# A distance table cut out of a shared buffer, and shorter declared form buffers, in a one-core attention + feed-forward kernel

## The chip, the cores and the metric

The kernel runs on one core of a Trainium2 chip. The metric is the device time of one execution in microseconds (us), as the median of several. A core has five engines that each take their own instructions in order: PE (TensorE, the matrix multiplier; its weight loads are shown as PEld), DVE (VectorE), ACT (ScalarE), POOL (GpSimd) and SP (SyncE, which here only issues transfers). They meet through semaphores: an instruction that waits holds up everything behind it on its engine.

## The reference

Sliding-window attention with a linear distance bias, for 8 batches, 8 heads, 576 positions and head size 64, followed by a two-matrix feed-forward layer with a squared ReLU:

```
scores = q @ k.T / sqrt(64)
scores = where(0 <= rel < 128, scores - slope[h] * rel, -1e9)     # slope[h] = 2**-(h+1)
attn   = softmax(scores);  x = (attn @ v), heads side by side     # 4608 x 512
out    = (max(x @ w_in, 0) ** 2) @ w_out                          # 512 -> 2048 -> 512
```

## The kernel before, in words

The 4608 rows are cut into nine chunks c of 512 columns, and the attention of a chunk into four couples (two heads each, p = 0 to 3). The feed-forward weights stay in SBUF in an "arena" of 16 places of 8 KB per partition (`w[f]`, f = 0 to 15: the first 4 KB for w_in, the other 4 KB for w_out, each split in a high and a low part so that a product is three matmuls).

**Stages.** In the start (to about 130 us) the weights are loaded and split and the first chunk is computed. Chunks 1 and 2 multiply directly (L318 and L356). From chunk 3 on, the first product uses a scheme with seven products of half size instead of eight (`product`, L410): its operands are sums of blocks of x, the "forms" B11, B21, B22, T1 to T4 (cast on ACT in L737, remainder on POOL through the helper `minus`, L341), and sums of blocks of the weights that come back from DRAM through a ring of five 2 KB buffers sum0 to sum4 (`load_sum`, L389). Forms of row 1 and some of row 0 lie in the first half of the odd places of the arena, whose w_in is no longer read then, while the second product (`second`, L356) goes on reading the w_out half of the same places.

**A couple.** PE computes scores into PSUM in a "visit" (L746, together with the values of an older couple, L767). DVE adds the distance table and takes row minima (`top`, L482). ACT takes the exponential (`exp`, L489), DVE the reciprocal of the sums (L503), POOL the normalization (`norm`, L514). DVE transposes blocks (L687), which go to DRAM (L693) and come back turned (L698) for the values of a later visit. From couple 8 on, one table of two heads serves all couples: before each couple ACT scales it in place by a power of two (`scale`, L206).

**Places.** In the last 24 KB per partition, `cst` holds the distance tables of all eight heads in 6 KB: heads 2 to 7 first, then heads 0 and 1, and `table` is the slice of the last 1.5 KB. When the tables of heads 2 to 7 are used up, their bytes are used again: the buffer sum0 ends in the first 1 KB of `cst`, and the buffer t30 (exponentials of a half couple, 3 KB) lies from byte 1536 to byte 4608 of it. So neither shares a byte with the slice `table`, but both share bytes with the declared tensor `cst`. The framework draws its waits between such named tensors. Every second couple uses t30 and t31, the others t0 and t1, which lie elsewhere.

**Order.** All engines have a written order that a planner makes with fixed costs and due times; it doesn't look at these waits.

Of the kernel before, what the change touches and what calls it, by code (L numbers as in the profile page):

```python
# [11 lines left out]
F32 = mybir.dt.float32  # L12
F32R = mybir.dt.float32r
# [8 lines left out]
B, H, S, D = 8, 8, 576, 64  # L22
# [48 lines left out]
CST = 128 + 192 * H  # L71
# [34 lines left out]
class Kern:  # L106
# [28 lines left out]
    def lay_out(self):  # L135
        parts = (
            ("x", 34816), ("pp", 8192), ("qk", 4608), ("v", 2560), ("t", 6144), ("h", 8192), ("r", 2048), ("o", 4096),
            ("y", 1024), ("t2", 3072), ("o2", 4096), ("qk2", 4608), ("h2", 4096), ("v2", 2560), ("cst", 6144),
        )
        self.nc.alloc_sbuf_tensor("rest", [128, sum(n for _, n in parts)], mybir.dt.uint8)  # L140
        at, self.home = self.nc.sbuf_base - sum(n for _, n in parts), {}
        for name, n in parts:
            self.home[name], at = at, at + n
        H = self.home
        many = lambda name, shape, dt, spots: Ring([self.at_byte(f"{name}{i}", shape, dt, a) for i, a in enumerate(spots)])
        self.lq = many("qk", [128, 1152], F32, (H["qk"], H["qk2"]))
        self.lv = many("v", [128, 5, 128], F32, (H["v"], H["v2"]))
        self.cst = self.at_byte("cst", [128, CST - 128], F32, H["cst"])
        self.table = self.cst[:, 1152:1536]
        self.tp = many("t", [128, 4, 192], F32, (H["t"], H["t"] + 3072, H["t2"]))  # L150
        self.op = many("o", [128, 2, 512], F32, (H["o"], H["o2"]))
        self.hp = many("h", [128, 2, 512], F32R, (H["h"], H["h"] + 4096, H["h2"]))
        self.hp.only(0, 1, 2)
        self.pp = many("pp", [128, 1024], F32, (H["pp"], H["pp"] + 4096))
        self.pp.only(0, 1)
        self.both = self.at_byte("both", [128, 2048], F32, H["pp"])
        self.r = self.at_byte("r", [128, 512], F32, H["r"])
        sums = H["t2"]
        self.r2 = self.at_byte("r2", [128, 512], F32, sums + 13312)
        self.u = self.at_byte("u", [128, 256], F32, sums + 15360)  # L160
        self.none = self.at_byte("none", [128, 256], F32, H["o2"])
        self.stage = self.at_byte("stage", [128, 4, 2, 256], F32R, sums)
        self.sr = many("sum", [128, 2, 256], F32R, [sums + i for i in (17408, 0, 2048, 4096, 6144)])
        self.sr.only(*range(5))
        self.o3 = self.at_byte("o3", [128, 512], F32, sums + 11264)
        self.o4 = self.at_byte("o4", [128, 2, 512], F32, sums + 13312)
        self.t3 = [self.at_byte(f"t3{i}", [128, 4, 192], F32, sums + at) for i, at in enumerate((19968, 8192))]
        dense = lambda name, slot, shape, dt: self.at_byte(name, shape, dt, H["x"] + 2048 * slot)
        self.xs = {(c, p): dense(f"x{c}{p}", 9 * c + 2 * p, [128, 2, 512], F32R) for c in range(2) for p in range(NP)}
        names = [(n, row) for row in range(2) for n in ("B11", "T1")] + [(n, 0) for n in ("B21", "B22", "T2", "T3", "T4")]  # L170
        odd = lambda f: self.arena + 8192 * f
        spots = [[H["x"] + 2048 * i for i in range(9)], [H["x"] + 2048 * (9 + i) for i in range(6)] + [odd(f) for f in (1, 3, 5)]]
        self.forms = [{}, {}]
        for c in range(2):
            for name, spot in zip(names, spots[c]):
                self.forms[c][name] = self.form(f"{name[0]}{name[1]}_{c}", spot)
        for i, n in enumerate(("B21", "B22", "T2", "T3", "T4")):
            self.forms[0][n, 1] = self.forms[1][n, 1] = self.form(f"{n}1", odd(2 * i + 7))
        two = lambda name, spot: self.at_byte(name, [128, 2, 256], F32, spot)
        self.far = [two(f"far{i}", H["x"] + 2048 * (15 + i)) for i in range(2)]  # L180
        self.tt = self.at_byte("tt", [128, 3, 256], F32, H["o"])
        self.near_x = two("now", H["o"] + 3072)

    def form(self, name, spot):
        if spot < self.home["x"]:
            return self.at_byte(name, [128, 2, 2, 512], F32R, spot)[:, 0, :, 0:256]
        return self.at_byte(name, [128, 2, 256], F32R, spot)

    def join(self, ctx):
# [9 lines left out]
        self.low, self.big = (ctx.enter_context(self.tc.tile_pool(name=n, bufs=1, space=PSUM)) for n in ("low", "big"))  # L199

    def near(self, h):
        h = (h - 2) % H
        return self.cst[:, 192 * h : 192 * (h + 1)]

    def scale(self, p):
        self.nc.scalar.activation(self.table, self.table, AF.Copy, scale=2.0**-2 if p else 2.0**6)  # L206
# [8 lines left out]
        self.nc.gpsimd.memset(self.tiny, 1e-9)  # L215

    def distances(self):
        self.nc.sync.dma_start(self.cst, self.cstd[:, 128:CST])

    def widen(self, p, queue=None):  # L220
        a = CST + 512 * p
# [1212 lines left out]
```

## Time and profile before

| what | us |
|---|---|
| median of 3 runs (lowest, highest) | 909.11 (907.0, 910.17) |
| the profiled execution's own time | 909.9 |
| its span, first to last instruction | 908.0 |
| PE busy | 867.9 (96%) |
| DVE, ACT, POOL busy | 464.0, 439.0, 454.5 |

The profile comes from one execution. A busy PE is the matmuls' own time, so the idle time between them is what waits cost; the granted TensorE clock is given as a share of 2.4 GHz. "Idle before <- X" in a row is the time the engine stood still just before the instruction, and the instruction whose end let it go.

### The profile page before, as it was taken

To read this page: it belongs to the slowest core of one execution; us is meant where nothing else is said; L and a number is where in the kernel's file an instruction comes from. 1 tells how busy PE (TensorE), PEld (TensorE's weight loads), DVE (VectorE), ACT (ScalarE), POOL (GpSimd) and SP (SyncE) were. 2 spreads that over 40 slices of the span, in tenths; PEclk is the share of its full clock that TensorE was granted. 3 is DMA by queue.
4 is the path that set the end of the run, shared out by engine and by line. 5 is a ranking of instruction groups with operands and counts; after the bars stand their busy time and mean duration, and the time that the engine had idled before them with its cause. 6 is when DMAs were issued, how large, how long until landed. Compare 5 with 4: busy or idle time off the path is not lost.

```text
span 908.0 us, 20552 instructions
## 1 busy us (share of the span) xinstructions
PE 867.9 (96%) x7644; PEld 776.8 (86%) x7648; DVE 464.0 (51%) x1492; ACT 439.0 (48%) x1195; POOL 454.5 (50%) x480
## 2 busy tenths in 40 slices
PE   8899999999999999998999989999999799999998
PEld 5688887888888898887999879888889699999997
DVE  6999964122323245555665445645555455434342
ACT  7898865555665554444444333434444444223111
POOL 4312115798896555565456445555446534543222
PEclk9999999999999999999999989999999899999999
DMA  9995465445656357664667647665766555734331
GB/s 339 403 330 196 140 175 181 141 153 179 226 190 221 117 178 241 202 205 154 203 225 227 199 160 234 201 206 183 253 202 208 172 162 193 224 134 142 111 111 47
DMA packets 95651, 176.39 MB, mean 194 GB/s; under 512 B 9088, under 2 KB 35008, under 8 KB 95552
## 3 DMA queue, kind: packets, MB, share of 16 engines
q1 hardware_dynamic: 85264, 165.31, 55.1%
q10 hardware_dynamic: 10288, 9.77, 3.6%
q8 instruction: 61, 1.00, 0.5%
q14 instruction: 38, 0.31, 0.1%
HBM read 135.07 MB, written 39.98 MB: 193 GB/s over the span
## 4 chain that ended last, share of the span: by engine, by line
PE 60%; DVE 8%; ACT 5%; POOL 5%; DMA 3%; issue 2%; SPq 0%; ACTq 0%; DVEq 0%; POOLq 0%
PE acc L356 28%; PE g L410 11%; PE s L410 8%; PE g L318 7%; DVE t L482 5%; PE s L767 3%; DMA sum<-sums 3%; PE g L746 3%; ACT t L489 3%; POOL h L341 2%; DVE both L687 2%; PE s L746 1%; POOL t L514 1%; POOL T L341 1%; POOL B L341 1%
## 5 line engine op out<-in xcount | busy, mean ns | idle before, releaser
L356 PE MATMUL acc<-h,w 128*128 128x512 f32 x1728 | 418.9, 386 | 9.9 <-POOL T L341 9.9
L356 PEld LDWEIGHTS acc<-h,w 128*128 128x128 f32 x1728 | 329.4, 199 | 44.2 <-POOL T L341 10.7
L341 POOL TENSOR_TENSOR h<-r,h 128x512 fp32r<-128x512 f32 x128 | 167.6, 1311 | 160.9 <-ACT h L439 143.2
L318 PE MATMUL g<-x,w 128*128 128x512 f32 x576 | 133.9, 382 | 5.9 <-ACT r L324 4.0
L489 ACT ACTIVATE t<-t,nm 128x192 f32<-128x192 f32 x256 | 114.4, 448 | 44.5 <-DVE nm L482 40.4
L318 PEld LDWEIGHTS g<-x,w 128*128 128x128 f32 x576 | 107.4, 189 | 25.5 <-ACT r L324 7.7
L482 DVE CUSTOM_DVE_ANT_0 t<-g,cst 128x192 f32<-128x192 f32 (+4 forms) x192 | 56.9, 313 | 136.2 <-PE g L746 125.4
L439 ACT CAST h<-r 128x512 fp32r<-128x512 f32 x96 | 59.2, 617 | 117.2 <-PE acc L356 76.0
L514 POOL TENSOR_TENSOR t<-t,nm 128x768 f32<-128x768 f32 x57 | 86.3, 1515 | 34.5 <-DVE nm L503 32.4
L410 PE MATMUL g<-B,w 128*128 128x256 f32 x576 | 81.1, 277 | 6.1 <-ACT u L419 6.1
L410 PEld LDWEIGHTS g<-B,w 128*128 128x128 f32 x576 | 76.0, 192 | 10.7 <-ACT u L419 8.2
L410 PE MATMUL s<-T,sum 128*128 128x256 f32 x576 | 80.4, 276 | 3.8 <-ACT cst L206 2.3
L434 DVE SCALAR_TENSOR_TENSOR r<-r 128x512 f32<-128x512 f32 x96 | 78.7, 820 | 7.3 <-ACT r L427 1.5
L410 PEld LDWEIGHTS s<-T,sum 128*128 128x128 f32 x576 | 75.1, 191 | 7.5 <-ACT cst L206 3.1
L417 DVE TENSOR_TENSOR u<-s,u 128x256 f32<-128x256 f32 x48 | 20.3, 422 | 104.4 <-PE s L410 98.7
L417 DVE TENSOR_TENSOR r<-g,u 128x256 f32<-128x256 f32 x96 | 40.6, 423 | 29.5 <-PE g L410 14.3
L687 DVE STREAM_TRANSPOSE both<-t 128x768 f32<-128x768 f32 x56 | 51.4, 955 | 2.1 <-PE s L767 2.0
L767 PE MATMUL s<-both,v 64*64 64x64 f32 (+1 forms) x1648 | 50.1, 243 | 0.2
L482 DVE CUSTOM_DVE_ANT_0 t<-s,cst 64x192 f32<-64x192 f32 (+4 forms) x142 | 41.3, 298 | 14.0 <-ACT t L489 10.8
L489 ACT ACTIVATION_READ_ACCUMULATOR t<-t,nm 128x1 f32 x256 | 48.0, 187 | 0.0
L341 POOL TENSOR_TENSOR tt<-now,far 128x256 f32<-128x256 f32 x12 | 8.8, 735 | 75.7 <-ACT now L725 75.7
L410 PE MATMUL g<-B,sum 128*128 128x256 f32 x288 | 40.8, 278 | 5.1 <-DVE r L417 4.0
(113 smaller groups left out, 1144.1 us busy)
## 6 DMA issues: line engine op xcount, KB each, us to landing
sum<-sums SPq DMA_DIRECT2D x192, 256.0 KB, 3.8
both<-way SPq DMA_DIRECT2D x28, 1024.0 KB, 6.9
raw<-in_dram SPq DMA_DIRECT2D x32, 512.0 KB, 7.9
qk<-in_dram SPq DMA_DIRECT2D x32, 320.0 KB, 3.1
v<-in_dram SPq DMA_DIRECT2D x32, 320.0 KB, 3.9
qk<-in_dram SPq DMA_DIRECT2D x36, 256.0 KB, 3.8
way<-both SPq DMA_DIRECT2D x56, 160.0 KB, 3.3
way<-both ACTq DMA_DIRECT2D x56, 160.0 KB, 3.5
```

Of the source, the lines that this page charges most:

```text
L318: nc.tensor.matmul(g, w, in_turn(xs[cc][:, part]), start=i == 0, stop=i == 11)
L341: return self.nc.gpsimd.tensor_tensor(to, a, b, op=op)
L356: self.nc.tensor.matmul(self.acc[m], w, in_turn(h), start=(f == 0 and i == 0), stop=(f == NF - 1 and i == 2))
L410: nc.tensor.matmul(to, w, in_turn(t[:, part]), start=i == 0 and k in (1, 5, 6, 7), stop=i == 5, skip_group_check=True,)
L417: V, add = nc.vector, lambda to, a, b: nc.vector.tensor_tensor(to, a, b, op=ALU.add)
L434: V.scalar_tensor_tensor(r, r, 0.0, r, op0=ALU.max, op1=ALU.mult)
L439: nc.scalar.copy(both[:, 0], r)
L482: self.nc.vector.tensor_tensor_reduce(self.t[r, m, a:e], spot, table[r, a:e], -0.125, least, ALU.add, ALU.min, to,)
L489: e = self.nc.scalar.activation(self.t[:, m], self.t[:, m], AF.Exp, bias=nm[:, m : m + 1], scale=-1.0, accum_out=nm[:, 4 + m : 5 + m],)
L514: self.nc.gpsimd.tensor_tensor(self.t, self.t, rec.unsqueeze(2).to_broadcast([128, 4, 192]), op=ALU.mult)
L687: nc.vector.transpose(squares[:, :, s].rearrange("p b m c -> p m b c"), G.t.rearrange("p m (b c) -> p m b c", c=32))
L767: made.append(mm(to, w, x, start=first and n < 2, stop=not first, skip_group_check=True))
```

## The change

The tables of heads 0 and 1 become a tensor `table` of their own, at the same bytes as the slice before, with their own load; `cst` is declared with 1152 columns, which end where t30 ends. The forms in the arena's odd places are declared 4 KB long instead of 8 KB, at the same bytes.

```diff
-        self.cst = self.at_byte("cst", [128, CST - 128], F32, H["cst"])
-        self.table = self.cst[:, 1152:1536]
+        self.cst = self.at_byte("cst", [128, 1152], F32, H["cst"])
+        self.table = self.at_byte("table", [128, 384], F32, H["cst"] + 4608)
...
         if spot < self.home["x"]:
-            return self.at_byte(name, [128, 2, 2, 512], F32R, spot)[:, 0, :, 0:256]
+            return self.at_byte(name, [128, 2, 512], F32R, spot)[:, :, 0:256]
...
     def near(self, h):
-        h = (h - 2) % H
-        return self.cst[:, 192 * h : 192 * (h + 1)]
+        table, h = (self.table, h) if h < 2 else (self.cst, h - 2)
+        return table[:, 192 * h : 192 * (h + 1)]
...
     def distances(self):
-        self.nc.sync.dma_start(self.cst, self.cstd[:, 128:CST])
+        self.nc.sync.dma_start(self.table, self.cstd[:, 1280:CST])
+        self.nc.sync.dma_start(self.cst, self.cstd[:, 128:1280])
```

The instructions of PE, DVE, ACT and POOL keep their order; SP has one transfer more. What differs is for what they wait. A row is one instruction with what it writes and reads; in brackets are the semaphores it waits for (DMAHWn is a transfer). Lines of the changed kernel are one higher.

On ACT, the stretch of the couple that is scored at 507 us. Before:

```order
L419 COPY u<-g 128x256 [waits PE_49]
L693 DMA way<-both 32x5x256 [waits DMAHW4_49,DMAHW6_49,DMAHW3_49,DVE_49]
L693 DMA way<-both 32x5x256 [waits DMAHW7_49]
L737 CAST T_133<-tt 128x256 [waits PE_49,Pool_49]
L489 ACTIVATE t_104,nm<-t_104,nm 128x192 x2
L206 ACTIVATE cst<-cst 128x384 [waits DMAHW0_49,Pool_49]
L427 ACTIVATE r<-g 128x256 [waits PE_49]
L737 CAST B_131<-now 128x256
L499 ACTIVATE nm<-nm,tiny 128x4 [waits Activation_49]
L737 CAST T_134<-tt 128x256 [waits PE_49]
L737 CAST B_132<-now 128x256 [waits PE_49]
```

And now:

```order
L420 COPY u<-g 128x256 [waits PE_49]
L694 DMA way<-both 32x5x256 [waits DMAHW7_49,DMAHW4_49,DVE_49]
L694 DMA way<-both 32x5x256 [waits DMAHW0_49]
L738 CAST T_134<-tt 128x256 [waits PE_49,Pool_49]
L490 ACTIVATE t_105,nm<-t_105,nm 128x192 x2
L206 ACTIVATE table<-table 128x384
L428 ACTIVATE r<-g 128x256 [waits PE_49]
L738 CAST B_132<-now 128x256
L500 ACTIVATE nm<-nm,tiny 128x4 [waits Activation_49]
L738 CAST T_135<-tt 128x256 [waits PE_49]
L738 CAST B_133<-now 128x256 [waits PE_49]
```

The scaling of the table waited for a transfer (the load of sum0) and for POOL (the normalization of t30), and now for neither.

On DVE, the tops of the same couple (t_103 is t30 and t_104 is t31 before; t_104 and t_105 after). Before:

```order
L482 ISA t_104,nm<-g,cst 128x128 [waits DMAHW6_49,DMAHW4_49,PE_49]
...
L482 ISA t_103,nm<-g,cst 128x192 [waits DVE_49]
...
L482 ISA t_104,nm<-s,cst 64x64 [waits DVE_49,Activation_49]
...
L482 ISA t_104,nm<-s,cst 64x64 [waits Activation_49]
...
L482 ISA t_104,nm<-s,cst,nm 128x64 [waits Activation_49]
L482 ISA nm 128x1
L482 ISA t_104,nm<-s,cst,nm 128x64
```

And now:

```order
L483 ISA t_105,nm<-g,table 128x128 [waits PE_49]
...
L483 ISA t_104,nm<-g,table 128x192
...
L483 ISA t_105,nm<-s,table 64x64 [waits Activation_49]
...
L483 ISA t_105,nm<-s,table 64x64
...
L483 ISA t_105,nm<-s,table,nm 128x64 [waits DVE_49]
L483 ISA nm 128x1
L483 ISA t_105,nm<-s,table,nm 128x64 [waits DVE_49]
```

Two waits of the tops for ACT (the exponentials of t30) and the first top's wait for a transfer are gone; one wait for ACT stays, for the copy that empties the bank.

On PE, the place where `second` first reads place 13 of the arena after the form T31 (T3 of row 1) was written there. Before:

```order
L410 MATMUL s_5659<-T40_0_121,w15_965 128x256 [waits DVE_49]
L410 MATMUL s_5659<-T40_0_121,w15_965 128x256 x2
L410 MATMUL s_5659<-T41_135,w15_965 128x256 x3
L356 MATMUL acc_4791<-h0_85,w13_909 128x512 [waits Pool_49]
L356 MATMUL acc_4791<-h0_85,w13_909 128x512 x2
```

And now:

```order
L411 MATMUL s_5661<-T40_0_122,w15_967 128x256 [waits DVE_49]
L411 MATMUL s_5661<-T40_0_122,w15_967 128x256 x2
L411 MATMUL s_5661<-T41_136,w15_967 128x256 x3
L357 MATMUL acc_4793<-h0_86,w13_911 128x512 [waits Pool_49]
L357 MATMUL acc_4793<-h0_86,w13_911 128x512 x2
```

Nothing moved here: the matmul on the w_out half of place 13 waits for POOL in both.

## Rows read from the trace of the kernel before

**Rows 1.** Busy time of each engine by stretch: start:end, length, engines, clock, DMA share.
```profile
128.00:344.93 216.93, 212.46 (x1800) 185.69 (x1796) 70.03 (x328) 125.40 (x328) 152.64 (x160) 1.00 0.54 177
344.93:790.12 445.19, 420.14 (x4107) 386.20 (x4106) 239.68 (x758) 182.18 (x563) 230.93 (x232) 0.98 0.63 202
446.58:492.74 46.16, 45.82 (x462) 42.32 (x462) 28.50 (x92) 20.02 (x63) 25.62 (x26) 1.00 0.68 221
525.29:531.00 5.71, 5.71 (x16) 4.63 (x17) 0.49 (x1) 0.58 (x3) 4.41 (x4) 0.53 0.04 15
723.20:729.00 5.80, 5.79 (x17) 4.72 (x18) 0.50 (x1) 0.67 (x3) 4.42 (x4) 0.53 0.10 36
```

**Rows 2.** Who waited for whom: us in total, times, longest.
```profile
ACT cst L206 <- DMA sum<-sums: 22.8, 7, 4.3
DVE t L482 <- ACT t L489: 20.7, 30, 1.4
PE acc L356 <- POOL T L341: 9.9, 3, 4.8
```

**Rows 3.** Timeline of PE: start, us, instruction, idle before.
```profile
408.12 0.94 PE L410 MATMUL g<-B,sum 128*128 128x256 f32 x6 [2.23 <-DVE r L417]
...
516.25 0.94 PE L410 MATMUL g<-B,w 128*128 128x256 f32 x6 [0.22 <-ACT u L419]
...
519.67 0.83 PE L410 MATMUL s<-T,w 128*128 128x256 f32 x6
525.29 5.48 PE L356 MATMUL acc<-h,w 128*128 128x512 f32 x12 [4.79 <-POOL T L341]
...
537.34 0.56 PE L746 MATMUL g<-qk 64*64 64x192 f32 x8
...
603.93 0.94 PE L410 MATMUL g<-B,sum 128*128 128x256 f32 x6 [0.88 <-DVE r L417]
...
723.21 5.49 PE L356 MATMUL acc<-h,w 128*128 128x512 f32 x12 [4.28 <-POOL T L341]
```

**Rows 4.** Timeline of ACT before the gap at 520 us.
```profile
517.25 0.44 ACT L489 ACTIVATE t<-t,nm 128x192 f32<-128x192 f32 x1
...
522.11 0.52 ACT L206 ACTIVATE cst<-cst 128x384 f32<-128x384 f32 x1 [4.33 <-DMA sum<-sums]
...
523.30 0.39 ACT L737 CAST T<-tt 128x256 fp32r<-128x256 f32 x1
```

**Rows 5.** Chain of waits before the same gap.
```profile
516.46 5.58 DMA sum<-sums
```

**Rows 6.** Timeline of DVE, tops of the couple scored at 507 us.
```profile
511.31 0.22 DVE L482 CUSTOM_DVE_ANT_0 t<-s,cst 64x64 f32<-64x64 f32 x1 [0.61 <-ACT t L489]
...
512.47 0.28 DVE L482 CUSTOM_DVE_ANT_0 t<-s,cst,nm 128x64 f32<-128x64 f32 x1 [0.61 <-ACT t L489]
```

**Rows 7.** Timeline of POOL before the gap at 520 us.
```profile
516.61 1.47 POOL L514 TENSOR_TENSOR t<-t,nm 128x768 f32<-128x768 f32 x1
518.04 0.73 POOL L341 TENSOR_TENSOR T<-tt,T 128x256 fp32r<-128x256 f32 x1
523.28 0.73 POOL L341 TENSOR_TENSOR B<-now,B 128x256 fp32r<-128x256 f32 x1 [4.51 <-ACT B L737]
```

**Rows 8.** Chain of waits before the gap at 603 us.
```profile
597.58 0.40 ACT B L737
...
602.18 1.24 POOL h L341
```

**Rows 9.** Timeline of SP: the table's load; a read of turned blocks.
```profile
13.38 0.33 SPq L218 DMA_DIRECT2D cst<-in_dram  x1
...
20.57 3.01 SPq L285 DMA_DIRECT2D raw<-in_dram  x2
...
519.54 0.37 SPq L698 DMA_DIRECT2D both<-way  x1
```

**Rows 10.** Page, transfers by line: times, KB each, median us to landing.
```profile
both<-way SPq DMA_DIRECT2D x28, 1024.0 KB, 6.9
```

## The prediction

> **What bounds the kernel now.** Read the busy time by stretch first. PE is what the end hangs on, and what it loses are its idle times: 216.93 − 212.46 = 4.47 us between 128 and 344.93 us, and 445.19 − 420.14 = 25.05 us between 344.93 and 790.12 us [rows 1], in which 18 couples are scored, one about every 23 to 27 us. In the quiet pair of couples from 446.58 to 492.74 us only 0.34 us are idle [rows 1]. So the second stretch has nine pairs, and 9 x 46.16 = 415.4 us would do for what takes 445.2: 29.8 us are lost there. Besides idle time these hold a slower clock: after the two longest gaps, 4.79 us before 525.29 and 4.28 us before 723.21 [rows 3], the granted clock is 0.53 for 5.71 and 5.80 us [rows 1], close to the lower level of 1.2 GHz. That costs 5.71 x 0.47 + 5.80 x 0.47 = 5.4 us.
>
> Then read who waits for whom. The scaling of the table on ACT (L206) waits 22.8 us in seven places for a load of weight sums, and DVE's tops wait 20.7 us in 30 places for ACT's exponentials [rows 2]. Neither makes sense for the data: a table doesn't need the sums, a top doesn't need an exponential. They come from sum0 and t30 lying in bytes of the declared `cst`. Then see in the chain whether PE feels it. Before the gap at 520 us the chain runs: load of sum0, issued at 516.46 and landed 5.58 us later [rows 5]; ACT, which was done with its exponentials at 517.69 and stood still for 4.33 us, scales at 522.11 and gets to the cast of T31 at 523.30 [rows 4]; POOL, idle for 4.51 us, takes B21 at 523.28 [rows 7] and then T31, for which PE waits at 525.29. Everything behind the scaling in ACT's queue (relu of the product, casts of the forms, casts of h) pays for a wait that isn't its own.
>
> **The change part by part.**
>
> *Table apart.* The order of waits shows the scaling waiting for nothing but its own engine's past, and the tops of t31 no longer for the exponentials of t30. I walk the gap at 520 us again with the rows' durations. The two waits of 0.61 us on DVE go [rows 6], so the last tops and ACT's exponentials end about 1.2 us sooner; the copy that PE waited 0.22 us for at 516.25 [rows 3] is then in time, and PE asks for T31 at 519.67 + 0.64 − 0.22 = 520.1 (six matmuls of 256 columns at 2.4 GHz follow each other in 0.64 us). ACT scales by 517.7 at the latest instead of 522.11. Relu, cast of B21, the small ACT step and the cast of T31 took 523.30 + 0.39 − 522.63 = 1.06 us together behind the scaling; the cast of T31 also needs the product that stands three such groups ahead of the one at 519.67, so started at 517.75 − 0.22 and ready 0.83 us later [rows 3], at 518.3, and ends at 518.7. POOL has T21 done by then, takes B21 from about 518.2 and T31 from 519.0, 0.73 us each [rows 7]: T31 is there at 519.75, before PE asks at 520.1. The 4.79 us go whole, by this walk, and with them the half clock. The other long gap has the same rows around it (idle 4.28 us [rows 3]); there I take the same. What is late next there is T41 and the two remainders of h on POOL, 0.73 and 2 x 1.27 us after a normalization of 1.47 [rows 7]: done at about 525.2, while PE needs the second h at about 526. That is within a microsecond, so a part of it may come back.
>
> The short gaps hang on the same two waits (copy u behind stalled exponentials, scaling behind POOL's normalization), except where forms come late by themselves. The gap of 0.88 us at 603.93 [rows 3] has a chain without either wait: cast of B22 at 597.58, then POOL without a pause to the end of h at 602.18 + 1.24 [rows 8]. It stays, and of the 2.23 us at 408.12 [rows 3], which has the same POOL work behind a late scaling, I leave as much.
>
> *Forms 4 KB long.* Nothing: PE's matmul on place 13 waits for POOL's T31 with the edit as without, since the weights of the place are still declared 8 KB. The three waits of `second` for a form, 9.9 us [rows 2], get shorter only by T31 coming sooner. If the edit did more than its waits show, at most what is left of these 9.9 us would go too.
>
> *Load in two.* The same 768 KB in two transfers. One more issue takes 0.33 us of SP's time [rows 9]. From below it costs nothing, as PE has other work; from above, each later weight load goes one place later, 3.01 / 2 = 1.5 us at that point [rows 9]. I take 0.4, nearer to the issue row: the second chunk's weights are wanted some 20 us later. The Trainium skill speaks against this edit: "DMA: Bandwidth & Descriptors", section "Rules for kernel authors", wants small transfers joined into one large one, and its section on latency gives some 2 us of fixed cost to a transfer. By the page, as an estimate, the sum below would be up to 2 us worse; no row here shows a fixed cost apart from landing times.
>
> The Trainium skill, "TensorE: Matmul & The Clock Gate", section "Why this matters for your kernels", says that a long idle gap between matmul bursts puts the array back to half rate. The trace agrees: 0.53 after 4.79 and 4.28 us.
>
> *Sum.* In the second stretch at the best pair's pace 29.8 us; less what stays, two POOL-bound gaps of 0.88 and about two short waits for T31 of 0.6 (the third of the 9.9 us has 0.8), each with some 0.27 us for the array to fill again, 4.0 together: 25.8. In the first stretch DVE and ACT stall each other in the same way behind the relu for which PE waits; of 4.47 us idle I take 3.9. Less 0.4 for the load: 29.3 us. The profiled execution took 909.9 us, 0.8 above the median of the runs: 909.1 − 29.3 = 879.8, so I say **880 us**.
>
> **The rivals.**
>
> *The real chain is right behind.* ACT and POOL work in a fixed order; if the products, not the scaling, hold the casts, a gap shrinks instead of closing. For it: the 0.88 us at 603.93 are such a gap, and the walk above left under 1 us to the remainders of h. Against it: ACT and POOL each stood still for over 4 us in the long gap [rows 4, 7]. If half of 25.05 us idle stays and the clock falls once instead of twice, the gain is 12.5 + 2.7 + 1 to 2 in the first stretch, some 17: 892 us.
>
> *The read of the turned blocks is late: slower.* The loads of sums held back by the scaling now go up to 4 us sooner, and run beside the blocks' way through DRAM. The read issued at 519.54 [rows 9] lands at about 526.4, with 6.9 us to land [rows 10]; PE uses it in the visit at 537.34 [rows 3], which would come some 8 us sooner, at about 529.5. So 3 us of slack are left. If other transfers took 5 us more from each read, PE would wait 2 us in each of 18 visits, 36 us, more than the 29 gained: about 915 us. It decides from 4.6 us on. Against it: with tops and transposes 1.2 us sooner the read goes out sooner as well, and the transfers' share is only 0.63 [rows 1].
>
> *No effect.* The waits that go may each stand beside a real one that ends at the same time; then 907 to 910 us. Against it speaks that the trace names the load itself as what ended ACT's 22.8 us.
>
> **How the numbers follow.** Forecast (870 to 888) 0.65, real chain behind (888 to 903) 0.24, no effect 0.05, slower 0.06. A difference of 0.3%, about 2.7 us, is what a measurement of this kernel can tell from none. Faster 0.90, same 0.05, slower 0.05 (a bit of each of the last two cases falls to its neighbour). The range is 872 to 896: below it would need nearly all 29.5 us of idle time, the clock and the filling to go at once (909 − 38), above it most of the real chain. The bounds of the extra load, 0 and 1.5 us, lie inside.
>
> **What would show it.** In the changed kernel's profile: the scaling has no idle time before it that a transfer or POOL's normalization ended, and tops have none that an exponential of the same couple ended; PE's gaps near 520 and 720 us are under 1 us and the clock stays at 1.00 throughout; the stretch from the first to the last visit runs at about 46 us per pair; the wait of `second` for T31 is still listed, smaller; an idle gap of about 0.9 us stays where the forms of an odd chunk are made. Wrong would be: new idle time on PE ended by the read of turned blocks or by POOL's h, of more than 5 us in all, or gaps in the first 90 us that grew by more than 1.5 us.

## The result and the profile after

The changed kernel takes **868.05 us** (median, 867.72 to 868.84), the kernel before 908.49 us in the same comparison: a ratio of 0.956, with a 95% interval of 0.954 to 0.958. The forecast was 880 us with a range of 872 to 896. The sign was right; the gain is 40.4 us where 29.3 were forecast, and the time lies below the range.

The profiled run has a span of 866.2 us against 908.0. From the page of the changed kernel, first the busy time per engine (share of the span, instructions), then PE's busy tenths and granted clock in 40 slices, the head of the chain that ended last, and two rows for transfers (what is moved, times, KB each, us to landing):

```profile
PE 854.9 (99%) x7644; PEld 773.9 (89%) x7648; DVE 460.1 (53%) x1492; ACT 435.9 (50%) x1195; POOL 455.9 (53%) x480
...
PE   9899999999999999999999999999999999999997
...
PEclk9999999999999999999999999999999999999999
...
PE 89%; POOL 3%; ACT 3%; DMA 3%; DVE 1%; issue 0%; SPq 0%; ACTq 0%
...
sum<-sums SPq DMA_DIRECT2D x192, 256.0 KB, 3.5
both<-way SPq DMA_DIRECT2D x28, 1024.0 KB, 6.5
```

PE is busy for 99% of the span and makes up 89% of the chain (60% before). The read of turned blocks lands in 6.5 us, not later than before (6.9 [rows 10]), so the rival that made the kernel slower has no ground.

By stretch, with the columns of [rows 1]. The first two rows are the same times as there, in which the changed kernel is already at later work; the third is the same pair of couples as 446.58 to 492.74 there:

```profile
128.00:344.93 216.93, 216.92 (x1836) 192.77 (x1833) 73.81 (x338) 127.71 (x338) 157.60 (x164) 1.00 0.57 186
344.93:790.12 445.19, 443.53 (x4389) 414.27 (x4388) 248.53 (x778) 188.25 (x578) 245.85 (x249) 1.00 0.66 212
429.87:475.30 45.43, 45.43 (x462) 42.28 (x462) 27.92 (x92) 19.76 (x64) 24.78 (x26) 1.00 0.69 224
```

Idle time of PE fell from 4.47 to 0.01 us in the first stretch and from 25.05 to 1.66 us in the second. The granted clock is 1.00 in both; the Trainium skill ("TensorE: Matmul & The Clock Gate", section "Why this matters for your kernels") ties the half rate to long idle gaps, and with the gaps the half rate went. The last section shows gaps behind which it went otherwise.

What PE still waits for, in the whole run, the four longest waits with a releaser (us in total, times, longest):

```profile
PE acc L357 <- POOL T L342: 1.3, 1, 1.3
PE g L250 <- DVE zero L230: 1.2, 1, 1.2
PE g L319 <- ACT r L325: 0.8, 1, 0.8
PE at L639 <- DMA qk<-in_dram: 0.7, 1, 0.7
```

Only the first lies behind 128 us; the other three are in the first 90 us. Of the 30 gaps of 0.2 us or more that PE had after 128 us before, this one is left.

The long gap of 520 us before [rows 3, 4, 7], in the changed kernel at the same work. ACT:

```profile
498.77 0.44 ACT L490 ACTIVATE t<-t,nm 128x192 f32<-128x192 f32 x1
499.12 0.18 ACT L490 ACTIVATION_READ_ACCUMULATOR t<-t,nm 128x1 f32 x1
499.21 0.51 ACT L206 ACTIVATE table<-table 128x384 f32<-128x384 f32 x1
...
500.62 0.41 ACT L738 CAST T<-tt 128x256 fp32r<-128x256 f32 x1
```

The scaling follows the last exponential at once, where it had stood 4.33 us for a load. POOL then has the last T at 501.10 + 0.73 = 501.8, and PE asks for it at 502.41:

```profile
501.74 0.83 PE L411 MATMUL s<-T,w 128*128 128x256 f32 x6
502.41 2.76 PE L357 MATMUL acc<-h,w 128*128 128x512 f32 x12
```

The walk in the prediction had put these 0.35 us apart; it is 0.6, and no gap of PE comes back behind it.

### The profile page after: what moved, and what is told of

Its sections match the earlier page's. It is cut to its first block, busy times and chain, and to the rows that moved or that the text cites. A ratio compares the mean times of both kernels' runs of the same rounds, so it can differ in the third digit from the quotient of the medians.

```text
span 866.2 us, 20509 instructions
## 1 busy us (share of the span) xinstructions
PE 854.9 (99%) x7644; PEld 773.9 (89%) x7648; DVE 460.1 (53%) x1492; ACT 435.9 (50%) x1195; POOL 455.9 (53%) x480
## 4 chain that ended last, share of the span: by engine, by line
PE 89%; POOL 3%; ACT 3%; DMA 3%; DVE 1%; issue 0%; SPq 0%; ACTq 0%
PE acc L357 41%; PE g L319 14%; PE g L411 13%; PE s L411 10%; PE s L768 4%; PE g L747 3%; PE s L747 1%; DMA table<-in_dram 1%; POOL B L342 1%; ACT t L490 1%; POOL h L342 1%; POOL T L342 1%; POOL t L515 1%; DMA wide<-in_dram 1%; PE at L589 1%; DMA ident<-in_dram 1%
## 5 line engine op out<-in xcount | busy, mean ns | idle before, releaser
L357 PE MATMUL acc<-h,w 128*128 128x512 f32 x1728 | 413.3, 382 | 1.3 <-POOL T L342 1.3
L490 ACT ACTIVATE t<-t,nm 128x192 f32<-128x192 f32 x256 | 114.0, 447 | 21.6 <-DVE nm L483 15.7
L483 DVE CUSTOM_DVE_ANT_0 t<-g,table 128x192 f32<-128x192 f32 (+4 forms) x192 | 54.4, 311 | 132.0 <-PE g L747 130.3
L325 ACT ACTIVATE r<-g 128x512 f32<-128x512 f32 x48 | 28.5, 593 | 35.1 <-PE g L319 31.4
L428 ACT ACTIVATE r<-g 128x256 f32<-128x256 f32 x48 | 18.3, 381 | 54.6 <-PE g L411 42.6
```

Source lines behind the costliest of these rows:

```text
L357: self.nc.tensor.matmul(self.acc[m], w, in_turn(h), start=(f == 0 and i == 0), stop=(f == NF - 1 and i == 2))
L483: self.nc.vector.tensor_tensor_reduce(self.t[r, m, a:e], spot, table[r, a:e], -0.125, least, ALU.add, ALU.min, to,)
L490: e = self.nc.scalar.activation(self.t[:, m], self.t[:, m], AF.Exp, bias=nm[:, m : m + 1], scale=-1.0, accum_out=nm[:, 4 + m : 5 + m],)
```

## Experiments

All differences below are between medians; "before" ran beside each of them, and each ratio has an interval of about 0.002 to either side (2 us). In the cuts of code, `behind(a, b)` makes instruction a wait for the end of b; lines that only keep a name for b are left out.

**Forms 4 KB long, alone.** In the kernel before only the declaration of the forms in the odd places is changed:

```
-            return self.at_byte(name, [128, 2, 2, 512], F32R, spot)[:, 0, :, 0:256]
+            return self.at_byte(name, [128, 2, 512], F32R, spot)[:, :, 0:256]
```

> Kernel before with the second part of the change alone: the forms in the odd weights' places are declared 4 KB long, the distance table stays a part of the constants. My theory: the tensor of the weights in which the form's write lands is still declared 8 KB, so TensorE's wait for GpSimd's form write stays, and nothing else had to do with the declared length: 908.5, as the kernel before, same gaps. Rival, that the shorter declaration carries part of the gain: below 904.

909.44 us, ratio 1.000 (0.999 to 1.002). The second part of the change gives nothing by itself, and with the table apart forms of 8 KB cost nothing either (868.21 us in the last experiment below); all of the gain is the table's.

**Which neighbour of the table was it?** `cst` shared bytes with two buffers, `sum0` and `t30`. One kernel gives the table a declared length that reaches over t30 and not over sum0, one adds the waits with sum0 alone by hand (cut short):

```
-        self.table = self.at_byte("table", [128, 384], F32, H["cst"] + 4608)
+        self.table = self.at_byte("table", [128, 1152], F32, H["cst"] + 1536)[:, 768:1152]
```

> Kernel after, but the table is the last third of a tensor declared 4608 bytes long that shares declared bytes with the buffer t30 and none with the buffer sum0; table, loads and arithmetic are the same. So only the false waits between table and t30 come back (tops for the exponentials of t30, those exponentials for the next tops, the scaling for GpSimd's norm of t30). My theory, by adding up the gaps of the kernel before that such a wait ends (12.3 us of idle time and about 18 refills of 0.26 us): 885, no gap above 3 us and no fall of the clock. Rival, the stalls of the sum0 load do it all: 868 to 870. Rival, t30's waits do nearly all: 903 or more.

```
+    def after_sum0(self, made):                       # called for each scaling and each top
+        if self.loaded: self.tc.add_manual_dep(made.ins, self.loaded.ins.name, SYNC, ...)
...
         made = self.nc.sync.dma_start(...)            # load of a weight sum
+        if to is self.sr.all[0]:
+            if self.scaled: self.tc.add_manual_dep(made.ins, self.scaled.ins.name, SYNC, ...)
+            self.loaded = made
```

> Kernel after with the waits between the table and the buffer sum0 added by hand (the load of sum0 waits for the last scaling of the table; scalings and tops wait for the last load of sum0); those with t30 stay gone. My theory, by the gaps of the kernel before that such a wait ends (15.7 us of idle time, 5.4 us of lowered clock behind the two long ones, about 10 refills of 0.26 us): 892, with the two gaps above 4 us near 520 and 710 us and the granted clock near 0.5 behind them. Rival, sum0 does it all: 905 or more. Rival, t30 does nearly all: 872 or less.

889.77 and 889.62 us: 21.7 and 21.6 us above the changed kernel, each near half of the 40.4; neither "one does it all" holds.

The first figure isn't t30's alone. In that kernel the table is declared over bytes of `cst` too, so the load of `cst` waits for the load of the table, and SP's queue with it. From SP's waits and PE's first projection in that run, and PE's in the changed kernel:

```profile
SPq L219 <- DMA table<-in_dram: 7.6, 1, 7.6
```

```profile
39.86 2.83 PE L319 MATMUL g<-x,w 128*128 128x512 f32 x12
```

```profile
35.90 2.83 PE L319 MATMUL g<-x,w 128*128 128x512 f32 x12
```

So PE is 4.0 us late there, and 4.1 at the first visit behind the start (139.55 us against 135.43), ahead of the first gap that t30's waits make (143.46). From there to the end the two profiles differ by 17.6 us, and that is t30's part; with the 21.6 of sum0 it makes 39.2 of the 40.4. So my 17 for t30 was right, though 885 for that kernel was not, and my 24 for sum0 was 2.4 too much. PE's gaps share out cleanly too: 1.3 us of idle time after 128 us in the changed kernel, 13.4 in 21 gaps with t30's waits, 15.7 in 11 gaps with sum0's, 28.8 in 30 gaps before. Three gaps of PE with t30's waits:

```profile
188.84 2.86 PE L319 MATMUL g<-x,w 128*128 128x512 f32 x12 [1.65 <-ACT r L325]
...
467.71 0.49 PE L411 MATMUL g<-B,w 128*128 128x256 f32 x2 [0.34 <-ACT u L420]
...
518.47 2.87 PE L357 MATMUL acc<-h,w 128*128 128x512 f32 x12 [0.79 <-POOL T L342]
```

And three with sum0's:

```profile
513.33 2.90 PE L364 MATMUL acc<-h,w 128*128 128x512 f32 x9 [3.95 <-POOL T L349]
...
590.06 0.94 PE L422 MATMUL g<-B,sum 128*128 128x256 f32 x6 [0.89 <-DVE r L429]
...
702.70 4.40 PE L364 MATMUL acc<-h,w 128*128 128x512 f32 x12 [3.32 <-POOL T L349]
```

t30 makes many short gaps, in nearly every pair of couples; sum0 makes few and long ones. The middle row of each matters below: the 0.34 us at 467.71 lie in the stretch that answers to the "quiet pair" of the prediction, and the 0.89 us at 590.06 are the gap of 603.93 [rows 3] that the prediction said had no false wait in it.

**sum0: which direction?** In one kernel only the load waits for the last scaling; in the other only scalings and tops wait for the last load.

```
+            self.behind(made, self.scaled)            # load_behind: at the load of sum0
```

> Kernel after with one of the two directions between the table and the buffer sum0: each load of sum0 waits for the last scaling of the table; scalings and tops wait for no load. With both directions the time was 889.6. Theory, the scaling that waits for the load does the harm, and the load's own wait for an earlier scaling is over when its turn comes: 868 to 870. Rival, the load's wait holds up SP's queue with all loads of sums behind it: 880 or more. Rival, the two directions make each other later, so that each alone costs less than half: 870 to 875.

```
+        self.behind(made, self.loaded)                # scale_behind: at each scaling and each top
```

> Kernel after with the other direction alone: scalings and tops of the table wait for the last load of sum0; the load waits for no scaling. Theory, this wait does the harm, since ACT's casts of the forms stand behind the scaling: 887 to 890, with the gaps of 3 to 4 us near 513 and 703 us. Rival, the loads themselves go earlier when they don't wait for a scaling, so this direction alone costs less than half: below 878.

867.73 and 888.81 us. The load's wait costs nothing; the other direction is all of sum0's part, and within it the scaling's wait, since no top of that run stands idle for a load. The rows of `scale_behind`, who waited for whom:

```profile
POOL B L349 <- ACT B L748: 25.6, 13, 5.0
ACT table L206 <- DMA sum<-sums: 23.3, 7, 4.1
```

The scaling waits 23.3 us in seven places, as before (22.8 [rows 2]), and POOL's remainders of the forms wait 25.6 us (5.9 in the changed kernel) for the casts that stand behind it in ACT's queue.

**t30: which waits?** Four steps: the tops with the exponentials; the scaling with GpSimd's norm; both; and the first with, added, 65 tops of t30 that wait for the end of DVE's own top before them.

```
+                    self.behind(made, self.powered)   # top: last exponential of t30
+            self.behind(e, self.topped)               # exponential of t30: last top
```

> Kernel after with the waits between tops and exponentials alone: tops wait for the last exponential in the buffer t30, and exponentials in t30 for the last top. With all of t30's waits the time was 889.8. Theory, by the gaps of that run that are put down to the relu r, the copy u and DVE's nm (16 gaps, 8.4 us idle, 0.27 us of refill each): 881. Rival, it is all of it: 888 or more. Rival, the scaling's wait for GpSimd's norm does most: below 873.

```
+        self.behind(made, self.normed)                # scaling: last norm of t30
```

> Kernel after with one wait of t30's alone: the scaling of the table waits for GpSimd's last norm of the buffer t30. Theory, by the gaps of the run with all of t30's waits that are put down to the form T or to a product behind the scaling (5 gaps, 3.8 us more idle than in the kernel after, 0.27 us of refill for each new one): 873. Rival, nothing, the norm is over when the scaling comes: 868. Rival, most of the 21.7 us: 883 or more.

> Kernel after with two of t30's waits together: tops with exponentials (878.6 alone) and the scaling with GpSimd's norm of t30 (868.1 alone). All of t30's waits gave 889.8, so 11 us are not explained by the one and the other alone. Theory, the norm of t30 ends late only where the exponentials were held up, so the scaling's wait bites only together with them: 885 to 890, with gaps of some 0.8 us put down to the form T near 510, 605 and 700 us. Rival, they add up: 879, and the rest is elsewhere, in the 65 tops of t30 that wait for DVE's own top before them.

```
+                    if self.t is self.K.t3[0]:        # with the two lines of tops_behind
+                        self.K.behind(made, self.K.topped)
```

> Kernel after with tops and exponentials waiting for each other (878.6) and, added to that, 65 tops that write t30 waiting for the end of DVE's own top before them, as a top that writes a tensor sharing bytes with the table it reads must. Theory that the scaling's wait for the norm is the missing 11 us: 879 to 880. Rival, DVE's own waits are: 885 to 890. By the time that DVE stands between two such tops in the run with all of t30's waits (0.12 us), 65 of them are 7.8 us of DVE's time, of which only what delays an exponential for which the copy u waits can count: 879 to 884.

878.62, 868.09, 882.06 and 882.84 us. So the tops' waits cost 10.6 us; the norm's wait costs nothing alone and 3.4 us beside them (the norm ends late only if the exponentials were held up); DVE's waits on itself cost another 4.2, in runs that spread over 3.6 us (880.24 to 883.83): the run with a mean granted clock of 1.000 took 880.24, the four at 0.998 took 882.72 or more, so about half of the 4.2 may be a lowered clock. The gaps of 0.8 us for the form T came as expected with the norm's wait (at 513.17, 605.72 and 698.99), but at 882.06 they are not the 11 us that I looked for, and DVE's own waits are not either; for these the estimate by DVE's time (879 to 884) held. My 873 for the norm alone was wrong, its rival "nothing" right. The 11 us were partly not there to find: 4.1 of them are the late load of `cst` shown above. The three steps together make 10.6 + 3.4 + 4.2 = 18.2 us beside t30's 17.6, which agrees within the spread; all three in one kernel, and the memsets and norms on GpSimd that waited for DVE's tops, were not tried. How DVE's own wait reads: two tops of t30 before,

```profile
610.23 0.36 DVE L482 CUSTOM_DVE_ANT_0 t<-g,cst 128x192 f32<-128x192 f32 x1
...
610.63 0.36 DVE L482 CUSTOM_DVE_ANT_0 t<-g,cst 128x192 f32<-128x192 f32 x1
```

and the same tops after:

```profile
582.74 0.35 DVE L483 CUSTOM_DVE_ANT_0 t<-g,table 128x192 f32<-128x192 f32 x1
...
583.01 0.35 DVE L483 CUSTOM_DVE_ANT_0 t<-g,table 128x192 f32<-128x192 f32 x1
```

0.40 us from start to start against 0.27: the wait shows as no idle time with a releaser, only as a longer step.

**What does a further load cost?** The constants in six transfers instead of one, on the changed kernel:

```
-        self.nc.sync.dma_start(self.cst, self.cstd[:, 128:1280])
+        for i in range(6):
+            self.nc.sync.dma_start(self.cst[:, 192 * i : 192 * i + 192], self.cstd[:, 128 + 192 * i : 320 + 192 * i])
```

> Kernel after with the constants' six other head tables loaded in six transfers of 98 KB in place of one of 590 KB: five more transfers on SP's queue, between the distance table and the loads of the first weights; the rest is the same. By the prediction's 0.4 us for each added load: 870. By the theory that an added load on this queue costs TensorE nothing, since no gap of TensorE in the first 90 us of the kernel after is put down to a weight that came late: 868. Rival, each transfer holds the queue up for some 2 us, so that the first weights and all that hangs on them start up to 10 us later: 872 to 878.

869.31 us (868.80 to 871.12): 1.26 more for five more transfers, 0.25 each. The two intervals overlap, so the trace has to say that there is a cost: SP spends 5.52 us on the six where one took 0.33, and PE's first projection starts at 37.61 instead of 35.90 us. SP's row:

```profile
13.89 5.52 SPq L220 DMA_DIRECT2D cst<-in_dram  x6
```

The rival of 2 us per transfer is out. That small transfers are better joined, as the Trainium skill says ("DMA: Bandwidth & Descriptors", section "Rules for kernel authors"), agrees in sign: 1.26 us for five.

**The wait that is left.** Place 13's weights are read by PE in their second half while GpSimd writes the form T31 into the first. In one kernel they are two tensors of 4 KB (the lines that then read the halves apart are left out here); in the next too, but the forms are declared 8 KB again.

```
+        if f == 13:
+            self.w[f] = [self.at_byte(f"w{f}{i}", [128, 2, 512], F32R, self.arena + f * 8192 + 4096 * i) for i in range(2)]
```

> Kernel after with the one odd weight place whose first half a form overwrites while its second half is still read (place 13) declared as two tensors of 4 KB, so that TensorE's reads of the second half no longer wait for GpSimd's write of the form; the cast and the subtraction of that place become two each (two instructions more). My theory: the wait of 1.3 us near 412 us goes with its refill of 0.3, and what stands behind it is not late: 866.5. Rival, the real chain through GpSimd's next form or norm is right behind: 868, with the gap near 412 put down to it. Rival, the two added instructions delay the first conversions and nothing else: 868.5.

> Place 13's weights as two tensors of 4 KB, as in the kernel of 866.5, but the forms in the odd places declared 8 KB again, so that a form's declared bytes reach into the second half. My theory: TensorE's reads of the second half wait for GpSimd's write of the form again, so the gap of 1.3 us near 412 us is back: 868. That would say that the shorter declaration pays only together with the split of the weights. Rival, the split alone did it: 866.5, no gap.

866.49 us (866.19 to 866.96) and 868.21 us (867.27 to 869.05). The gap of the changed kernel,

```profile
412.30 2.22 PE L357 MATMUL acc<-h,w 128*128 128x512 f32 x9 [1.30 <-POOL T L342]
```

is gone with the split, though T31 itself is no earlier; PE starts at 410.45, before POOL begins the remainders T at 411.35:

```profile
410.45 2.76 PE L371 MATMUL acc<-h,w 128*128 128x512 f32 x12
```

```profile
411.35 1.86 POOL L356 TENSOR_TENSOR T<-tt,T 128x256 fp32r<-128x256 f32 x2
```

With the longer forms it is back, to the digit:

```profile
412.69 2.22 PE L371 MATMUL acc<-h,w 128*128 128x512 f32 x9 [1.30 <-POOL T L356]
```

The times of the split kernel lie below all those of the changed one (867.72 to 868.84), though the two intervals against the kernel before overlap; with the gap there and gone I take the difference as shown. So the shorter declaration is worth about 1.6 us, but only once the weights it lies in are declared apart as well. The kernel of 866.49 us is the fastest here: ratio to the kernel before 0.954 (0.952 to 0.956).

## Why the prediction was right in kind and short in size

I compare by when PE starts the same work. The changed kernel leads by 0.52 us at the end of the start (135.95 us before), by 7.07 at the visit of 336.51 before (329.44 after), by 42.24 at the visit of 782.14 (739.90), and by 41.8 at the end. These are two single executions, and the kernel before alone spreads over 3 us. Against the terms of the sum:

| stretch | forecast | measured |
|---|---|---|
| start, with the added load | −0.4 | +0.52 |
| first stretch | 3.9 | 6.55 |
| second stretch | 25.8 | 35.17 |
| end | 0 | −0.44 |
| together | 29.3 | 41.8 |

*The mechanism was right.* The waits of the scaling and the tops were false, they bound PE, and the walk through the gap at 520 us came out to within 0.3 us. The forms' part was worth nothing, as said.

*The step that failed most: "the second stretch at the best pair's pace".* I took the pair from 446.58 to 492.74 as what the kernel would run at without false waits, 46.16 us. It was not free of them. The changed kernel takes 45.43 us for the same pair with the same 462 matmuls. Two experiments show whose waits they are: with sum0's waits alone those at 428.26 and 473.68 stand 45.42 apart, as after (45.41), and with t30's waits alone those at 435.36 and 481.51 stand 46.15 apart, as before (46.15). The two stretches, first with sum0's waits, then with t30's:

```profile
428.26:473.68 45.42, 45.42 (x463) 42.27 (x456) 28.35 (x94) 19.93 (x62) 22.19 (x22) 1.00 0.69 233
```

```profile
435.36:481.51 46.15, 45.81 (x463) 42.33 (x456) 28.40 (x94) 20.36 (x62) 23.07 (x22) 1.00 0.70 229
```

The quiet pair was a pair without sum0 in it, and had t30's waits in full. Over nine pairs 9 x 0.73 = 6.6 us were missing. Its 0.34 us of idle time stood in the row I quoted, and I let it stand as pace; the other 0.39 were in PE's busy time, 45.82 against 45.43.

*The second: "two POOL-bound gaps of 0.88 that stay, two short waits for T31", 4.0 us.* Of these only the 1.30 us at 412.30 with a refill stayed, 1.6. I read the chain before 603.93 as free of false waits because it began at the cast of B22, 597.58 [rows 8]. The chain goes back to one releaser per step, and here it went to a step r of DVE, which ended at 597.57, 0.01 us before the cast:

```profile
597.14 0.43 DVE r L417
```

On ACT's own timeline, which the prediction didn't read there, the row ahead of that cast is:

```profile
597.15 0.52 ACT L206 ACTIVATE cst<-cst 128x384 f32<-128x384 f32 x1 [2.89 <-DMA sum<-sums]
597.58 0.39 ACT L737 CAST B<-now 128x256 fp32r<-128x256 f32 x1
```

That the scaling did hold the cast is shown twice: the gap is back at 590.06 (0.89) with sum0's waits alone, and after the change the cast starts 2.9 us before that step of DVE:

```profile
567.93 0.51 ACT L206 ACTIVATE table<-table 128x384 f32<-128x384 f32 x1
568.35 0.39 ACT L738 CAST B<-now 128x256 fp32r<-128x256 f32 x1
```

```profile
571.27 0.41 DVE L418 TENSOR_TENSOR r<-s,u 128x256 f32<-128x256 f32 x1
```

The second stretch was 9.4 us short. The two steps make 6.6 + 2.4 = 9.0 of that (the 2.4 are the 4.0 less the 1.6 that stayed).

*The third: the first stretch.* All of the 4.47 us idle went, not 3.9, and each of the six gaps had a refill that I had counted in the second stretch only: 4.47 + 6 x 0.27 = 6.1 of the 6.55 measured. The 0.27 itself had no row behind it in the prediction; the runs bear it out, as the last section shows.

*The load:* 0.4 charged, 0.25 by the experiment, and not the up to 2 us of the other estimate; nothing hangs on it. *The range:* I shut out "all idle time, the clock and the filling at once (909 − 38)" as its lower end. That is just what happened: 28.8 us idle, 5.4 of clock and 7.6 of PE's own busy time make up the 41.8. Of the signs that I named, the scaling and the tops without false waits, the clock at 1.00, the pace and the smaller wait for T31 came; the remaining 0.9 us where an odd chunk's forms are made did not.

## What to carry to other kernels

In this framework a buffer that is declared longer than what is used draws waits from whatever lies in the rest of its bytes; the waits look like real ones in the profile, so ask of each long wait whether its data needs it, and look which declared extents overlap. Don't take the best stretch of a kernel as its floor before you have looked for the suspected wait in that stretch too, and follow a chain on the engine's own timeline one row further back than the chain goes. A wait that costs nothing alone (the norm's) can cost something beside another, so a set of waits is best taken away whole and split by experiment. And an experiment that brings a wait back by laying one tensor over another brings every other wait of that overlap with it: compare its start with the kernel it came from before you read its time.

## What the runs showed that was not expected

- PE loses more than its idle time at each wait: with t30's waits, 12.1 us more idle time in 20 more gaps went with 17.6 us more from the first visit to the end, at full clock. That is 0.27 us beyond the idle time for each gap. By [rows 3], six matmuls behind a wait take 0.94 us instead of 0.83; where the rest goes isn't shown.
- While PE worked, the lower clock came only behind gaps of 2.2 us or more, and their length alone doesn't say behind which. With the scaling's wait alone (`scale_behind`), 3.99 us of idle time were followed by a clock of 0.54 for 5.7 us, and 3.36 us by none:

```profile
513.30:519.00 5.70, 5.70 (x17) 4.64 (x17) 0.50 (x1) 0.60 (x3) 4.41 (x4) 0.54 0.04 14
704.27:707.00 2.73, 2.73 (x13) 2.49 (x14) 0.49 (x1) 0.40 (x2) 2.73 (x3) 1.00 0.21 76
```

  With both directions (`sum0_waits`) a gap of 3.32 us was followed by 0.50 for 2.3 us. A gap of 2.25 us for the same form T stands in four profiles of t30's waits. In three of them the clock stayed at 1.00; with tops and norm together it fell, and the nine matmuls behind the gap took 3.78 us instead of 2.22:

```profile
419.41 3.78 PE L364 MATMUL acc<-h,w 128*128 128x512 f32 x9 [2.25 <-POOL T L349]
```

```profile
419.50:422.00 2.50, 2.50 (x7) 2.06 (x8) 0.00 (x0) 0.00 (x0) 1.78 (x2) 0.58 0.86 343
```

  Behind 2.21 us before 34.60 in the run with all of t30's waits, a gap that the changed kernel doesn't have, it was 0.50 from 36 to 38 us; that is a part of the 4.1 us by which that run is late. What sets these apart isn't shown.
- A wait of an engine for its own last instruction has a price where the data didn't ask for it: 0.13 us between the two tops of t30 shown above, and 65 tops wait in this way.
